# Wqkv in four chunks of 128 rows, a new lead for the first block, and new orders on all engines

## The chip, the core and the metric

The kernel runs on one core of a Trainium2 chip. A core has five engines that run their own instruction lists in order and wait for each other by semaphores: TensorE (PE, matrix products), VectorE (DVE), ScalarE (ACT), GpSimd (POOL) and SyncE (SP), which here issues all DMA transfers. The metric is the time of one execution on the device in microseconds (us), the median of several runs.

## The reference

The input x has 2048 rows of 512 bfloat16 numbers. The result is the sum of x, a sliding attention and a gated feed-forward layer, both of the normalised x:

```python
xn = _layernorm(x, axis=-1)
return x + _A_ref(xn, A_wqkv, A_wo) + _B_ref(xn, B_w_gate, B_w_up, B_w_down)
```

`_A_ref` makes Q, K and V with one weight matrix `wqkv` of 512 x 1536, splits them into 32 heads of 16 numbers, and lets each row attend to itself and seven earlier rows at a distance of two (offsets 0, 2, ..., 14). A softmax over the eight logits weighs V, and `wo` follows. `_B_ref` is `(gelu(xn @ w_gate) * (xn @ w_up)) @ w_down` with a hidden width of 1376.

## The kernel before

**Tiling.** The 2048 rows are worked in four blocks b of 512 rows, each made of four row tiles t of 128. The normalised x of a block lies transposed in `xnT`, features on partitions, so that a product takes 128 columns of a weight as the stationary side and up to 512 rows of x as the moving side. A product over the 512 features is four matrix instructions, kt = 0 to 3, one for each 128 features. PSUM has 8 banks of 512 float32 numbers a partition; every result takes a bank until ACT or DVE has read it.

**The steps of a block and their names.** A name is the step, the block, and a column group or a tile.
- Normalisation: `bnst`, `bnag`, `sub`, `sq`, `rstd`, `norm`. For the first four tiles the statistics are on DVE and the square root `sq0` to `sq3` on ACT; tile 1 has its sums on ACT (`sx1`, `negm1`, `sxx1`). Tiles 8 and later are normalised on ACT, with the power on POOL.
- Transposes: in block 0 by PE (`tpx`, line 899), read out by ACT (`evx`, line 919) and for tiles 0 and 1 half by DVE (`evy`, line 911). In the later blocks by DMA (`trx`, issued by SP).
- Q, K and V: in block 0, Q and K are made tile by tile as soon as a tile is transposed (`mma0_0`, `mmt0_t` for Q and `mmt1_t` for K, 128 columns each, line 959), V by 512 rows (`mm0_2_g`, line 1009). In the later blocks all three are `mm<b>_<which>_<g>`, by 512 rows. ACT reads them out (`evq`, `evk`, `evv`).
- Logits: DVE multiplies Q with shifted K (`pr`, line 1040) and adds (`pa`); PE sums over the numbers of a head (`er`, lines 1078 and 1085, which also makes a tail of the up projection); the softmax is `mask`, `d1` to `d6` on DVE with `exp`, `ln` and `d5` on ACT.
- The weights of attention go to DRAM and come back spread over the heads (`ss`, `sl` on SP). DVE multiplies them with shifted V (`pv`), adds (`pw`) and folds (`pz`).
- Feed-forward: `fg` and `fu` on PE (line 1221), `gelu` and `uev` on ACT, `h` on DVE.
- Output: `acc` on PE (line 1306, Wd and Wo), in the last block the part with Wo apart as `accw`; `fe` on ACT, `fin` on DVE, `sto` on SP.

**What sets the order.** Each engine's order is written out by hand in `ORDER` (line 404). `schedule` (line 207) walks through these lists with a table of costs only to give out PSUM banks and other buffers; `assign_sync` puts in the waits. An engine takes its list strictly in order, so a step that waits holds up all behind it.

**Around the change.** ACT's list begins with `c_tbl`, a square root of a constant that brings the square root's table (line 668), then `sx1 sq0 negm1 sxx1 sq1 evx0_0 evx0_1 evq0_0 sq2`. SP's begins with x of tiles 0 and 1, `ld_wq`, tile 2 of x, `ld_wk`, tile 3 of x, `ld_wv` and further x; the large load of the gate weights `ld_wg0` waits until `ld_wk` has landed (line 698), and stands on SP behind an x load that waits for PE. PE's begins with dummy products `warm0` to `warm14` on constants (line 678).

Of the kernel before, what the change touches and what calls it, by code (L numbers as in the profile page):

```python
# [21 lines left out]
    HAM_TAU=4.0,
    HAM_ENTER=0.52,
    HAM_EXIT=0.30,
)


class PeClock:

    def __init__(self, prm):  # L30
        self.tau = prm["HAM_TAU"]
        self.enter = prm["HAM_ENTER"]
        self.exit = prm["HAM_EXIT"]
        self.f = prm["PE_COLD_F"]
        self.avg = 0.0
        self.t = 0.0
        self.warm = False

    def run(self, start, dur, util):
        import math  # L40
        if start > self.t:
            self.avg *= math.exp(-(start - self.t) / self.tau)
            if self.warm and self.avg < self.exit:
                self.warm = False
            self.t = start
        left = dur
        total = 0.0
        while left > 1e-9:
            step = min(left, 0.2)
            real = step * (1.0 if self.warm else self.f)  # L50
            a = math.exp(-real / self.tau)
            self.avg = self.avg * a + util * (1.0 - a)
            if not self.warm and self.avg > self.enter:
                self.warm = True
            elif self.warm and self.avg < self.exit:
                self.warm = False
            total += real
# [78 lines left out]
class Graph:  # L136
# [70 lines left out]
    def schedule(self, orders, params=None):  # L207
        prm = dict(PARAMS)
        prm.update(params or {})
        LAT_X, LAT_S = prm["LAT_X"], prm["LAT_S"]  # L210
# [56 lines left out]
        for _ in range(len(self.tasks)):  # L267
# [23 lines left out]
            elif t.eng == "pe":  # L291
                sw = 0.0
                if t.mode is not None:
                    if pe_mode not in (None, t.mode):
                        sw = prm["PE_MODE_SWITCH"]
                    pe_mode = t.mode
                t.end = est + sw + pe_clock.run(est, t.dur, t.util)
                t.done = t.end + prm["PE_DRAIN"]
            else:
                t.end = est + t.dur  # L300
                t.done = t.end + prm["DRAIN"]
                if t.eng == "act" and t.table is not None:
                    act_table = t.table
# [85 lines left out]
    def report(self):  # L389
# [17 lines left out]
        "warm14 mma0_0 tpx0_1 mmt0_0 mmt0_1 mmt1_0 tpx1_0 mmt1_1 mmt0_2 tpx1_1 mmt1_2 mmt0_3 mmt1_3 "  # L407
        "mm0_2_2_0 mm0_2_1_0 fg0_0 mm0_2_0_0 fg0_1 fg0_2 fg0_3 fu0_0 fu0_1 mm0_2_3_0 fg0_4 fu0_2 fu0_3 fu0_4 "
        "fg0_5 mm1_1_0_0 mm1_0_0_0 fu0_5 fg0_6 er0_3 mm1_0_1_0 mm1_1_1_0 fg0_7 mm1_1_3_0 mm1_0_2_0 mm1_2_3_0 "
        "fg1_0 mm1_0_3_0 mm1_1_2_0 fg1_1 fu1_0 fu1_1 fu0_6 fu0_7 fg1_2 fu1_2 mm1_2_2_0 mm1_2_1_0 fg1_3 fu1_3 "  # L410
        "fg0_8 fg1_4 fu0_8 mm1_2_0_0 fg1_5 fg0_9 fu1_4 fu0_9 fu1_5 fg1_6 fg0_10 fu1_6 mm2_0_0_0 mm2_1_0_0 "
        "mm2_1_1_0 mm2_0_2_0 er1_3 fg1_7 mm2_0_3_0 mm2_0_1_0 fg1_8 mm2_1_3_0 mm2_2_0_0 fg2_0 mm2_1_2_0 accd2 "
        "fu1_7 accd1 mm2_2_2_0 fu1_8 acca0 fg1_10 mm2_2_3_0 accb0 fg2_1 fg2_2 accd3 fg2_3 fu2_0 fg1_9 fu2_1 "
        "mm2_2_1_0 fu2_2 fu2_3 er2_3 mm3_1_0_0 mm3_1_3_0 fu1_9 mm3_0_0_0 mm3_1_2_0 mm3_0_2_0 mm3_2_1_0 "
        "mm3_0_1_0 mm3_1_1_0 fg3_0 mm3_0_3_0 fg2_4 mm3_2_0_0 mm3_2_2_0 mm3_2_3_0 fu3_0 fu2_4 fg2_5 fg2_10 "
        "accd7 fu2_5 fg3_1 fu3_1 fg3_2 accd5 acca4 er3_3 fg2_6 accb4 accd6 fu2_6 fg2_7 fg2_8 fg3_10 fu2_7 "
        "fu3_2 fu2_8 fg3_3 fg3_4 fu3_3 fg3_5 fg2_9 fu2_9 fu3_4 fg3_6 fu3_5 fg3_7 fu3_6 fu3_7 fg3_8 fg3_9 "
        "fu3_8 accd11 acca8 accd10 fu3_9 accd9 accb8 acca12 accd13 accd14_0 accd14_1 accw14_0 accw14_1 "
        "accw13 accd15_0 accb12 accw15_0 accw12 accd15_1 accw15_1 accd15_2 accw15_2",
    "act":  # L420
        "c_tbl sx1 sq0 negm1 sxx1 sq1 evx0_0 evx0_1 evq0_0 sq2 evq0_1 evk0_0 evx1_0 sq3 evk0_1 bnst8 evx1_1 "
        "bnst9 evq0_2 evk0_2 evq0_3 evk0_3 ve8 sq6 vp8 sq4 bnag8 evv0_2_0 evv0_1_0 halo1 bnag9 evv0_0_0 va8 "
        "gelu0_0 bnst10 gelu0_2 uev0_0 bnst11 ve10 evv0_3_0 gelu0_1 vp10 gelu0_3 uev0_3 uev0_1 bnag10 "
        "evk1_0_0 evq1_0_0 gelu0_5 bnag11 gelu0_4 uev0_5 uev0_4 uev0_2 vb8 evq1_1_0 evk1_1_0 gelu0_6 gelu0_7 "
        "exp0 sub8 va10 evq1_2_0 vb10 ln0 sub11 d5_0 evk1_3_0 evq1_3_0 evv1_3_0 uev1_0 evk1_2_0 sub9 uev1_1 "
        "uev0_6 uev0_7 gelu1_1 gelu1_0 evv1_1_0 sub10 norm9 uev0_10b gelu1_3 evv1_2_0 gelu0_8 norm10 norm8 "
        "uev1_2 gelu1_2 norm11 gelu1_5 uev1_3 gelu1_4 bnst12 gelu0_9 uev0_9 uev1_5 uev0_8 uev0_10a bnst13 "
        "uev1_6 uev0_10c evv1_0_0 evq2_0_0 gelu0_10 evk2_1_0 ve12 evk2_0_0 vp12 evq2_2_0 bnag12 gelu1_6 "
        "uev1_4 evq2_3_0 gelu1_7 bnag13 evq2_1_0 halo2 evk2_3_0 exp1 bnst14 va12 bnst15 vb12 ve14 evk2_2_0 "
        "vp14 uev1_10b bnag14 ln1 uev1_7 d5_1 sub13 halv1 fe2 bnag15 uev1_8 va14 vb14 sub15 sub12 fe1 "  # L430
        "uev1_10c evv2_2_0 sub14 norm12 norm13 fe0 evv2_3_0 evv2_0_0 gelu2_2 gelu2_1 norm14 fe3 norm15 halo3 "
        "uev1_10a gelu2_0 gelu1_10 uev2_1 evv2_1_0 uev2_0 uev2_3 uev2_2 gelu1_8 uev2_10b uev2_10c gelu2_3 "
        "gelu1_9 evq3_0_0 evk3_0_0 evq3_2_0 evk3_3_0 evk3_2_0 evq3_1_0 exp2 halv2 evk3_1_0 uev1_9 evv3_0_0 "
        "evv3_3_0 ln2 evv3_2_0 evq3_3_0 d5_2 evv3_1_0 uev3_0 halv3 gelu2_5 uev2_10a gelu2_4 uev2_5 uev2_4 "
        "uev3_1 fe5 gelu2_10 gelu3_1 fe7 fe4 uev3_10c gelu3_2 gelu3_0 exp3 uev3_10b uev2_6 uev2_7 fe6 ln3 "
        "uev3_2 d5_3 uev2_8 gelu2_6 uev3_3 gelu2_7 gelu2_9 uev2_9 gelu2_8 gelu3_4 gelu3_5 uev3_5 gelu3_3 "
        "gelu3_6 uev3_6 uev3_4 uev3_7 gelu3_7 fe11 gelu3_10 fe10 gelu3_9 uev3_10a uev3_9 gelu3_8 uev3_8 fe8 "
        "fe9 fe13 fe12",
# [30 lines left out]
def d_act(n):  # L469
    return 0.10 + 0.00085 * n  # L470
# [950 lines left out]
```

## Time and profile before

| what | us |
|---|---|
| median of 3 runs (lowest, highest) | 184.19 (184.12, 184.24) |
| span of the profiled execution, first to last instruction | 182.8 |
| median less that span: what lies around it | 1.4 |
| PE busy | 178.0 |
| DVE busy | 168.8 |
| ACT busy | 129.3 |
| DMA, share of 16 engines over the span (queue 1) | 36.3% |

The page gives the span but no time of its own for the profiled execution, so the median of the runs stands for it. In a line of a timeline the first number is the start, the second the length, both in us from the span's start; then engine, line of the kernel, operation, output and input, and how many instructions are merged. Brackets name how long the engine stood idle just before and what ended it. Neighbouring instructions of an engine overlap a little at their ends, so that starts are the safer reading than lengths.

### The profile page before, as it was taken

The page shows a single profiled execution, that of the slowest core. Times are in us where ns is not written, and L with a number is a line of the kernel's source. Part 1 is how long each engine was busy: PE and PEld are TensorE (multiplying, and loading weights), DVE is VectorE, ACT ScalarE, POOL GpSimd, SP SyncE. Part 2 cuts the span into 40 slices and gives each one's busy share as a digit, 9 for nine tenths or more (in the row PEclk, how much of TensorE's full clock was granted, in tenths as well). Part 3 has the DMA queues.
Part 4 walks back from the last instruction along what each step waited for, and adds up shares of the span by engine and source line. Part 5 has one row for each costly group of instructions (what it writes and reads, how often), then busy time and mean ns, then how long its engine had stood idle before and what let it go on. Part 6 is the DMA issues. An engine that isn't in the chain of part 4 may idle for free.

```text
span 182.8 us, 2777 instructions
## 1 busy us (share of the span) xinstructions
PE 178.0 (97%) x1060; PEld 89.8 (49%) x1060; DVE 168.8 (92%) x169; ACT 129.3 (71%) x266; POOL 11.1 (6%) x23
## 2 busy tenths in 40 slices
PE   8799999999999999999999999999999999999994
PEld 2685444554444544444444555444444444444673
DVE  3769999999999999999999989999999999999932
ACT  5589977899899899869997596934396764145011
POOL 6000000104000000504000000000000000000000
PEclk9999999999999999999999999999999999999999
DMA  4999559610364000002742000136310246222333
GB/s 111 359 376 377 132 113 299 211 50 21 97 190 98 0 0 0 4 14 74 201 115 61 0 0 0 37 81 158 129 59 0 46 138 221 57 84 74 91 106 107
DMA packets 26220, 19.60 MB, mean 107 GB/s; under 512 B 13824, under 2 KB 23008, under 8 KB 26208
## 3 DMA queue, kind: packets, MB, share of 16 engines
q1 hardware_dynamic: 26208, 19.44, 36.3%
q8 instruction: 8, 0.13, 0.3%
q14 instruction: 4, 0.03, 0.1%
HBM read 14.71 MB, written 3.15 MB: 98 GB/s over the span
## 4 chain that ended last, share of the span: by engine, by line
PE 89%; DMA 8%; SPq 1%; issue 0%; DVE 0%; DVEq 0%
PE PS L1221 38%; PE PS L1306 28%; PE PS L1009 18%; DMA Wg<-in_B_w_gate_dram 5%; DMA Wqkv<-in_A_wqkv_dram 3%; PE PS L1260 2%; PE PS L1085 2%; PE PS L1078 1%; SPq L731 1%; SPq L687 0%; DVE OB L1350 0%; DVEq L376 0%
## 5 line engine op out<-in xcount | busy, mean ns | idle before, releaser
L1306 PE MATMUL PS<-Wd,HT 128*128 128x512 bf16 (+2 forms) x209 | 40.8, 345 | 0.0
L1221 PE MATMUL PS<-xnT,Wg 128*128 128x512 bf16 x160 | 39.6, 379 | 0.3 <-DMA Wg<-in_B_w_gate_dram 0.3
L1221 PE MATMUL PS<-xnT,Wu 128*128 128x512 bf16 x160 | 38.8, 379 | 0.0
L1009 PE MATMUL PS<-xnT,Wqkv 128*128 128x512 bf16 x160 | 37.8, 379 | 0.0
L1040 DVE TENSOR_TENSOR UNI<-QT,KT 128x4096 f16<-128x4096 bf16 x16 | 36.4, 2287 | 0.1
L1188 DVE TENSOR_TENSOR UNI<-VN,PT 128x4096 f16<-128x4096 bf16 x16 | 36.0, 2286 | 0.0
L1306 PEld LDWEIGHTS PS<-Wd,HT 128*128 128x128 bf16 x209 | 19.7, 98 | 19.0
L1238 ACT ACTIVATE UU<-PS 128x512 bf16<-128x512 f32 x40 | 22.8, 604 | 7.9 <-PE PS L1221 6.2
L1197 DVE TENSOR_TENSOR UNI<-UNI 128x4096 f16<-128x4096 f16 x12 | 27.4, 2286 | 0.0
L1009 PEld LDWEIGHTS PS<-xnT,Wqkv 128*128 128x128 bf16 x160 | 17.9, 114 | 16.9 <-ACT UU L1238 0.4
L1231 ACT ACTIVATE GG<-PS 128x512 bf16<-128x512 f32 x40 | 23.4, 600 | 2.5 <-DVE HT L1245 1.7
L1221 PEld LDWEIGHTS PS<-xnT,Wg 128*128 128x128 bf16 x160 | 15.4, 98 | 19.6 <-DMA Wg<-in_B_w_gate_dram 0.7
L1221 PEld LDWEIGHTS PS<-xnT,Wu 128*128 128x128 bf16 x160 | 15.7, 98 | 18.8
L1339 ACT ACTIVATE OB<-PS 128x512 bf16<-128x512 f32 x14 | 8.2, 594 | 21.8 <-PE PS L1306 21.8
L1053 DVE TENSOR_TENSOR UNI<-UNI 128x4096 f16<-128x4096 f16 x9 | 20.4, 2282 | 0.0
L1306 PE MATMUL PS<-Wo,OT 128*128 128x512 bf16 (+2 forms) x76 | 16.5, 345 | 0.0
L1245 DVE TENSOR_TENSOR HT<-GG,UU 128x1024 bf16<-128x1024 bf16 x20 | 13.6, 686 | 0.0
L832 POOL TENSOR_TENSOR sq<-ve,mhalf 128x2 bf16<-128x2 f32 x4 | 8.2, 2058 | 73.3 <-ACT ve L828 73.3
L1020 ACT ACTIVATE VN<-PS 128x512 bf16<-128x512 f32 x16 | 9.3, 594 | 2.5 <-PE PS L1009 2.5
L1306 PEld LDWEIGHTS PS<-Wo,OT 128*128 128x128 bf16 x76 | 7.2, 98 | 6.5
L1020 ACT ACTIVATE QT<-PS 128x512 bf16<-128x512 f32 x12 | 7.2, 597 | 3.2 <-PE PS L1009 3.2
L959 PE MATMUL PS<-xnT,Wqkv 128*128 128x128 bf16 x128 | 8.2, 219 | 1.2 <-DMA Wqkv<-in_A_wqkv_dram 1.0
(85 smaller groups left out, 153.9 us busy)
## 6 DMA issues: line engine op xcount, KB each, us to landing
PT<-pt_scratch SPq DMA_DIRECT2D x16, 256.0 KB, 4.0
XR<-in_A_x_dram SPq DMA_DIRECT2D x16, 128.0 KB, 2.4
out_dram<-OB SPq DMA_DIRECT2D x14, 128.0 KB, 2.0
Wqkv<-in_A_wqkv_dram SPq DMA_DIRECT2D x3, 512.0 KB, 5.6
XIN<-in_A_x_dram SPq DMA_DIRECT2D x6, 256.0 KB, 6.0
Wg<-in_B_w_gate_dram SPq DMA_DIRECT2D x1, 1280.0 KB, 8.8
Wu<-in_B_w_up_dram SPq DMA_DIRECT2D x1, 1280.0 KB, 11.6
Wd<-in_B_w_down_dram SPq DMA_DIRECT2D x1, 1280.0 KB, 7.7
```

Source lines behind the costliest of these rows:

```text
L832: "pool", "sq%d" % t, 7.0, lambda e, t=t, n=n: e.tensor_tensor(out=sq[:, t:t + n], in0=ve[:, t:t + n], in1=mhalf[:, 0:n], op=ALU.pow),
L1009: ins = e.matmul(PS[:, 512 * it.slot:512 * it.slot + 512], lhsT=wcols(which, kt, g), rhs=xnT[:, itx.slot, kt, :], start=(kt == 0), stop=(k ...
L1020: return e.activation(out=o, in_=PS[:, 512 * it.slot:512 * it.slot + 512], func=ACTF.Identity, scale=(QSC, 1.0, 1.0)[which])
L1040: return lambda e: e.tensor_tensor(out=UNI[:, it.slot, :, :], in0=bass.AP(QT, (itq.slot * 4 + g) * 512, [[NQT * 4 * 512, 128], [0, 8], [1, ...
L1053: return lambda e: e.tensor_tensor(out=UNI[:, i0.slot, :, :], in0=UNI[:, i0.slot, :, :], in1=UNI[:, i1.slot, :, :], op=ALU.add)
L1188: return lambda e: e.tensor_tensor(out=bass.AP(UNI, ito.slot * 4096, [[NUNI * 4096, 128], [2048, 2], [512, 4], [1, 512]]), in0=bass.AP(VN, ...
L1197: return lambda e: e.tensor_tensor(out=UNI[:, i0.slot, :, :], in0=UNI[:, i0.slot, :, :], in1=UNI[:, i1.slot, :, :], op=ALU.add)
L1221: ins = e.matmul(PS[0:M, 512 * it.slot:512 * it.slot + 512], lhsT=Wx[:, kt, j * 128:j * 128 + M], rhs=xnT[:, itx.slot, kt, :], start=(kt = ...
L1231: return lambda e: e.activation(out=GG[:, ito.slot, q, :], in_=PS[:, 512 * it.slot:512 * it.slot + 512], func=ACTF.Gelu_apprx_tanh)
L1238: return lambda e: e.activation(out=UU[:, ito.slot, q, :], in_=PS[:, 512 * it.slot:512 * it.slot + 512], func=ACTF.Identity)
L1245: return lambda e: e.tensor_tensor(out=HT[:, ito.slot, j - 1:j + 1, :], in0=GG[:, ig.slot, :, :], in1=UU[:, iu.slot, :, :], op=ALU.mult)
L1306: ins = e.matmul(PS[:, 512 * it.slot:512 * it.slot + CW], lhsT=(OT[:, ito.slot, q, ti * 128:(ti + 1) * 128] if kind == "o" else HT[:, ith. ...
```

## The change

Four things are changed, all in one step.

1. Wqkv is loaded in four transfers of 128 rows with all 1536 columns (`ld_w0` to `ld_w3`) in place of three of 512 rows by 512 columns. `ld_wg0` and `ld_wu0` wait for `ld_w1`.
2. For tiles 0 and 1, Q, K and V are made together, one chunk of 128 features at a time: `lk<kt>_<t>` is 12 matrix instructions of 128 columns, for three results in three banks. Tiles 2 and 3 have Q and K as before (`mmt`), and their V by 256 rows (`mmv_0`, `mmv_1`, 8 instructions of 256 columns each). ACT reads V of block 0 out in four pieces (`evv0_0`, `evv0_1`, `evv0_h0`, `evv0_h1`).
3. The costs that `schedule` uses are replaced and its model of PE's clock is dropped; this bears on the kernel only through which buffers are given out and where waits are put.
4. All engines but POOL have new orders; the set of instructions on DVE is the same as before. On ACT, `c_tbl` moves from the first place to the ninth, behind `sq2`, and `evx0_0` stands ahead of `sq1`. On SP, `ld_w0 ld_w1` follow tiles 0 and 1 of x, and `ld_x2` is the last x load ahead of the gate weights. On PE, steps of the blocks are interleaved in another way.

The core of the diff:

```diff
     "pe":
         "warm0 warm1 warm2 warm3 warm4 warm5 warm6 warm7 warm8 warm9 tpx0_0 warm10 warm11 warm12 warm13 "
-        "warm14 mma0_0 tpx0_1 mmt0_0 mmt0_1 mmt1_0 tpx1_0 mmt1_1 mmt0_2 tpx1_1 mmt1_2 mmt0_3 mmt1_3 "
-        "mm0_2_2_0 mm0_2_1_0 fg0_0 mm0_2_0_0 fg0_1 fg0_2 fg0_3 fu0_0 fu0_1 mm0_2_3_0 fg0_4 fu0_2 fu0_3 fu0_4 "
+        "warm14 lk0_0 tpx0_1 lk1_0 lk0_1 lk1_1 lk2_0 tpx1_0 lk2_1 lk3_1 tpx1_1 lk3_0 mmt0_2 mmt1_3 mmt0_3 "
+        "mmt1_2 mmv_1 fg0_0 fg0_1 fg0_2 fg0_3 mmv_0 fu0_0 fu0_1 fu0_2 fu0_3 fg0_4 mm1_0_0_0 fu0_4 mm1_1_0_0 "
...
     "act":
-        "c_tbl sx1 sq0 negm1 sxx1 sq1 evx0_0 evx0_1 evq0_0 sq2 evq0_1 evk0_0 evx1_0 sq3 evk0_1 bnst8 evx1_1 "
-        "bnst9 evq0_2 evk0_2 evq0_3 evk0_3 ve8 sq6 vp8 sq4 bnag8 evv0_2_0 evv0_1_0 halo1 bnag9 evv0_0_0 va8 "
+        "sx1 sq0 negm1 sxx1 evx0_0 sq1 evx0_1 sq2 c_tbl sq3 evx1_0 bnst8 evq0_1 evx1_1 evq0_0 bnst9 evk0_1 "
+        "sq6 evk0_3 evk0_0 evq0_2 sq4 evq0_3 evk0_2 ve8 vp8 bnag8 evv0_0 gelu0_0 bnag9 gelu0_2 sub8 gelu0_3 "
...
     "dve":
-        "sub7 pr0_1 rstd6 rstd4 norm7 norm5 norm6 pr0_0 norm4 pr0_3 pr0_2 pa0_0 pa0_1 pr1_0 mask d1_0 h0_1 "
+        "sub4 norm6 norm7 rstd4 norm5 norm4 pr0_3 pr0_1 pr0_0 pr0_2 pa0_0 h0_1 pa0_1 pr1_0 mask d1_0 rstd8 "
...
     "sp":
-        "ld_x0_0 ld_x0_1 ld_wq ld_x1_0 ld_wk ld_x1_1 ld_wv ld_x2 ld_x4 ld_x3 ld_wg0 ld_wu0 ld_wt0 ld_wt1 "
+        "ld_x0_0 ld_x0_1 ld_w0 ld_w1 ld_x1_0 ld_x1_1 ld_w2 ld_w3 ld_x4 ld_x3 ld_x2 ld_wg0 ld_wu0 ld_wt0 ld_x5 "
...
-        for i, nm in enumerate(("q", "k", "v")):
+        for i in range(4):
             def mk(i=i):
-                return lambda e: e.dma_start(
-                    Wqkv[:, :, i * 512:(i + 1) * 512],
-                    A_wqkv[:, i * 512:(i + 1) * 512].rearrange("(k p) n -> p k n", p=128))
+                return lambda e: e.dma_start(Wqkv[:, i, :], A_wqkv[128 * i:128 * i + 128, :])
...
-            t_w.deps.add(t_ld["wk"])
+            t_w.deps.add(t_ld["w1"])
...
+                def lead_mm(nm, gs, items, t, n, kts, rd, start):
+                    def f(e):
+                        ins = None
+                        for kt in kts:
+                            for (which, g, it, c) in gs:
+                                ins = e.matmul(PS[:, 512 * it.slot + c:512 * it.slot + c + n],
+                                               lhsT=wcols(which, kt, g),
+                                               rhs=xnT[:, XTI[0].slot, kt, t * 128:t * 128 + n],
+                                               start=(kt == 0 and c == 0), stop=(kt == 3 and c + n == 512))
+                        return ins
...
+                for t in range(2):
+                    its = [Item("mmt%d_%d" % (w_, t), P_ps, "qkv") for w_ in range(3)]
+                    for kt in range(4):
+                        lead_mm("lk%d_%d" % (kt, t), [(w_, g_, its[w_], 128 * g_) for w_ in range(3) for g_ in range(4)],
+                                its, t, 128, (kt,), xrd[t] + [(I_wq, kt)] + (its if kt else []), kt == 0)
```

## The prediction

> **What bounds the kernel now.** I read the page's busy times first, then the groups, PE's and ACT's first 30 us in order of time, and DVE's end.
>
> ```profile
> span 182.8 us, 2777 instructions
> PE 178.0 (97%) x1060; PEld 89.8 (49%) x1060; DVE 168.8 (92%) x169; ACT 129.3 (71%) x266; POOL 11.1 (6%) x23
> ```
>
> PE is the bound, and DVE is close behind it. PE's own timeline shows where its missing time is:
>
> ```profile
> 0.83 4.10 PE L678 MATMUL PS<-const-bfloat16-1.0 128*128 128x512 bf16 x10 [0.83 <-PEq L1406]
> 4.98 0.41 PE L899 MATMUL PS<-ident,XIN 128*128 128x128 bf16 x4
> 5.23 0.45 PE L678 MATMUL PS<-const-bfloat16-1.0 128*128 128x128 bf16 x5
> 6.65 0.39 PE L959 MATMUL PS<-xnT,Wqkv 128*128 128x128 bf16 x4 [0.97 <-DMA Wqkv<-in_A_wqkv_dram]
> 6.87 0.39 PE L899 MATMUL PS<-ident,XIN 128*128 128x128 bf16 x4
> 7.10 2.62 PE L959 MATMUL PS<-xnT,Wqkv 128*128 128x128 bf16 x44
> 9.55 0.39 PE L899 MATMUL PS<-ident,XIN 128*128 128x128 bf16 x4
> ...
> 17.17 1.04 PE L1221 MATMUL PS<-xnT,Wg 128*128 128x512 bf16 x4 [0.25 <-DMA Wg<-in_B_w_gate_dram]
> ```
>
> The reader is to see that dummy matmuls fill PE to 4.93, that the first useful product starts at 6.65 behind the Q weights, and that 44 products of 128 columns take 9.55 - 7.10 = 2.45 us, 55.7 ns each. The chain of waits gives the rate of the long ones:
>
> ```profile
> 19.07 4.32 PE PS L1221 x20
> ```
>
> That is 216 ns for each product of 512 columns. ACT's timeline holds the head of the chain that feeds PE, and a table load later on:
>
> ```profile
> 0.79 1.28 ACT L668 ACT_TABLE_LOAD   x1 [0.79 <-PEq L1406]
> 3.43 0.63 ACT L760 ACTIVATE XR<-XIN 128x512 bf16<-128x512 bf16 x1 [1.14 <-DMA XIN<-in_A_x_dram]
> 3.96 0.18 ACT L760 ACTIVATION_READ_ACCUMULATOR XR<-XIN 128x1 f32 x1
> 4.06 0.28 ACT L786 ACTIVATE sq<-mv,eps 128x1 bf16<-128x1 bf16 x1
> 5.51 0.36 ACT L919 ACTIVATE xnT<-PS 128x256 bf16<-128x256 bf16 x1
> ...
> 19.61 0.20 ACT L800 ACTIVATE vb<-s 128x2 bf16<-128x2 f32 x1
> 19.82 1.28 ACT L1231 ACT_TABLE_LOAD   x1
> 21.11 0.60 ACT L1231 ACTIVATE GG<-PS 128x512 bf16<-128x512 f32 x1
> ```
>
> The first load ends at 2.07, before x is there (3.43): it costs nothing. The one at 19.82 stands between two instructions and costs its whole 1.29 us. Last, DVE's end, from the timeline of all engines:
>
> ```profile
> 172.12 1.22 DVE L1203 TENSOR_TENSOR OT<-UNI 128x2048 bf16<-128x2048 f16 x1
> ...
> 173.65 1.51 PEld L1306 LDWEIGHTS PS<-Wo,OT 128*128 128x128 bf16 x12
> ```
>
> This is `pz3`, and after it the first product that needs it: DVE delivers 0.3 us before PE asks. A later DVE moves the end as surely as a later PE.
>
> **The change part by part.** The sum is against the profiled execution: span 182.8; the median of the three times is 184.19, so 1.4 us lie around the span, and I leave them as they are.
>
> *The head of ACT.* `c_tbl`, whose square root had the table loaded at 0.79, moves behind `sq2`. ACT's first instruction is now `sx1`, an Identity, and the built program has two loads ahead of `sq0`: one of another set before `sx1`, and one of the square root's set between `sx1` and `sq0` (eleven loads in all, ten before). The second can't start before `sx1` and its accumulator read are through, 4.14. With the 1.28 of the row, `sq0` goes from 4.06 to 5.44: +1.38. The chain behind it moves along: `norm0` 4.57 to 5.95, the transpose `tpx0_0` 4.98 to 6.36. `evx0_0` now stands ahead of `sq1` and so follows its transpose by the 0.45 that `evy0_0` had (5.43 against 4.98): 6.81, with 0.36 to 7.17. The first product `lk0_0` starts 0.07 later, 7.24 against 6.65: +0.59. The old wait for the Q weights is hidden behind this.
>
> [...]
>
> *The chunks of Wqkv.* The three loads of 512 KB become four of 384 KB in longer rows, the same bytes. The first two are issued one place earlier than K was. Ahead of chunk 0 are only 256 KB of x; K, with more in front of it, landed at 8.35. The products ask for chunk 0 at 7.24, 1 at 8.2, 2 at 10.2, 3 at 11.8: I cost it at nothing; what hides it is the later head. If a chunk were late, it costs PE its lateness, at most 1 us. `ld_x2` now waits for the transposes on SP with Wg and Wu queued behind: Wg goes out near 8.9, not 8.37. It landed at 17.13 and is asked for at 17.8: nothing, at worst 0.3.
>
> *The lead on PE.* Block 0's Q, K, V took 128 x 55.7 ns + 16 x 216 ns = 10.6 us; now 160 x 55.7 ns + 16 of 256 columns (half of 216, an estimate) = 10.65: +0.1. But the order leaves PE fewer gaps. From 6.65 to `er0_3` at 32.02 are 25.37 us; the work in them is 140 x 55.7 ns + 76 x 216 ns = 24.2, so PE stood for 1.15. In the new order I carried the three engines forward by hand with the rows' durations (512 evictions 0.5 from start to start, statistics 0.62, squares 0.70): PE waits once, 0.1, for `norm1` (sq1 7.07, norm1 done 7.94, `tpx0_1` 8.0). Then 172 x 55.7 ns + 16 x 108 ns + 64 x 216 ns = 25.1 give `er0_3` at 7.24 + 0.1 + 25.1 = 32.45, with one more group of four 512-products (0.86) done than before. So PE is 0.86 - 0.43 = 0.4 us ahead there. The covers are thin: `fg0_4` is due at 25.6 and its bank (`uev0_2`) free at 25.4; `pa0_1` is done at 32.3, just before `er0_3`. ACT stands at almost no idle from 11.6 to 40; a slip of 0.3 there costs PE 0.1 to 0.3.
>
> *DVE.* Its long stream began at `pr0_1`, 16.48. Now the evictions of Q and K end with `evk0_2`, done at 18.3, and four norms stand ahead of `pr0_3`: it begins at 18.35. In return two reciprocals and four norms (1.24 us, 18.69 to 19.67 and 21.87 to 22.13) are out of the stream, and the 0.9 us of waits that the profile names in it (0.3 for `er0_3`, 0.6 for the exponential) may go. `pz3` starts at 18.35 + (172.12 - 16.48) - 1.24 - 0.9 = 171.85 plus what DVE waits. PE, 0.4 ahead, wants it started by about 172.1. Up to 0.3 us of DVE waits are free, all above them move the end.
>
> *The orders behind it.* The instructions are the same; the waits are not. Bounds: none (the sums above), or what small misfits add up to. I carried PE's and DVE's sums through the new order without gaps: `er2_3` is due at 89.5 and its last addend `pa2_1` done at 89.0 (before: done at 87.1, asked for at 98.0); `h1_4` ahead of it asks for `uev1_9` in the moment it is ready; `d1_3` is 0.3 early for `er3_3`. The nearest rows for such misfits are the waits of DVE above, 0.3 to 0.6. I take 0.8 us on DVE or PE, 0.3 of which are free: +0.4, between 0 and 2. SP carries stores and transposes between the score loads, 0.3 to 1.3 us each; the multiplications they feed come 8.5 us and more behind the scores, as before: 0 to 0.3.
>
> Sum: +0.59 +0.1 -1.15 +0.1 = -0.4, and +0.4 for misfits: no change, 184.2.
>
> **The rivals.**
> 1. *Gapless.* All covers hold: -0.4 us, 183.8, and 183.5 with a head 0.3 quicker. For it: no engine in my sums is late by over 0.3 us. Against: six places have a slack under 0.3.
> 2. *The load is not in the way.* If `sq0` starts at 4.06 as before, `lk0_0` starts near 5.95, and 1.3 us come off the head: 182.9. Against: the built order has the load between `sx1` and `sq0`.
> 3. *Slower: DVE becomes the bound.* The place is `pa2_1` ahead of `er2_3`: PE there has nothing to cover it, and what DVE loses then is lost for `pz3` too. It decides from 1.1 us of DVE waits after 18.35 (0.3 free, 0.4 that PE is ahead, 0.4 to leave "no change"). With 2 us, as three waits of the length of those named, 184.2 - 0.4 + 1.7 = 185.5.
> 4. *Slower: PE falls back to its slow clock in the head.* Nine dummy products take 4.1 us, over 0.4 us each, twice the later 216 ns; PE warmed up at about 4.9. It now stands from 4.93 to 6.36 and again 0.35, against 0.97 at a stretch before, which slowed nothing. A fall that lasts as long as that warming, 4.1 us at half speed, costs 2.0: 186.2. [...]
>
> **How the numbers follow.** 0.2% is 0.37 us, about what a measurement of this kernel can tell from no change. No change as summed: 0.41, own range 183.85 to 184.55. Gapless 0.14, load not in the way 0.05: faster 0.19. DVE the bound or several small waits of PE 0.35, clock 0.05: slower 0.40. The range leaves out 1 in 10 on each side: down to the gapless 183.6, up to 185.6.
>
> **What would show it.** Two table loads before 5.5 us, the second 1.28 us at 4.14; `lk0_0` at 7.2; no wait of PE for Wqkv; `pr0_3` at 18.4; `er0_3` at 32.4 to 32.8; `pz3` at 172 to 173. I am wrong if `lk0_0` starts before 6.7 or after 7.6, if products near 8 us take over 60 ns each, or if PE's waits after 33 us come to more than 1 us.

## The result, and the profile after

The changed kernel takes 187.4 us (median of 4 runs, 186.25 to 187.58) against 184.22 for the kernel before on the same chip: 1.0156 times as long, 95% interval 1.0128 to 1.0184. I had forecast no change, 184.2, with a range that ended at 185.6. From the page of the profiled execution:

```profile
span 185.6 us, 2829 instructions
...
PE 177.7 (96%) x1075; PEld 92.4 (50%) x1092; DVE 169.6 (91%) x169; ACT 129.6 (70%) x267; POOL 8.4 (5%) x23
...
q14 instruction: 5, 0.04, 0.1%
```

The span grew by 2.8 us, while PE is busy 0.3 us less than before and DVE 0.8 more. The last line is from the list of DMA queues: five packets of instructions against four before; it becomes important below. ACT's timeline of the first 8 us:

```profile
0.80 1.28 ACT L713 ACT_TABLE_LOAD   x1 [0.80 <-PEq L1358]
3.71 0.63 ACT L713 ACTIVATE XR<-XIN 128x512 bf16<-128x512 bf16 x1 [1.63 <-DMA XIN<-in_A_x_dram]
4.24 0.19 ACT L713 ACTIVATION_READ_ACCUMULATOR XR<-XIN 128x1 f32 x1
4.45 1.28 ACT L739 ACT_TABLE_LOAD   x1
5.74 0.30 ACT L739 ACTIVATE sq<-mv,eps 128x1 bf16<-128x1 bf16 x1
...
7.11 0.38 ACT L872 ACTIVATE xnT<-PS 128x256 bf16<-128x256 bf16 x1
```

The second load stands where it was expected, between `sx1` and `sq0`, and takes 1.28 us with nothing behind it: 5.74 follows 4.45 + 1.28 at once. All of it is some 0.3 later than forecast, because this execution's x came 0.28 later (3.71 against 3.43). PE in the same stretch, and then, as the last line, the start of `er0_3`, the first step behind the lead:

```profile
6.68 0.40 PE L852 MATMUL PS<-ident,XIN 128*128 128x128 bf16 x4 [2.13 <-DVE mv L716]
6.91 0.45 PE L635 MATMUL PS<-const-bfloat16-1.0 128*128 128x128 bf16 x5
7.55 1.47 PE L910 MATMUL PS<-xnT,Wqkv 128*128 128x128 bf16 x12 [0.18 <-ACT xnT L872]
8.81 0.63 PE L852 MATMUL PS<-ident,XIN 128*128 128x128 bf16 x4
9.24 3.61 PE L910 MATMUL PS<-xnT,Wqkv 128*128 128x128 bf16 x48
12.69 0.39 PE L852 MATMUL PS<-ident,XIN 128*128 128x128 bf16 x4
...
34.37 0.62 PE L1030 MATMUL PS<-xnT,Wt 128*32 128x256 bf16 x16
```

PE stands 2.13 us, and then the first 12 products of the lead take 8.81 - 7.55 = 1.26 us, 105 ns each, twice the 55.7 of before; the 48 behind them average 72. The table of stretches says why. Its columns are the stretch, its length, the busy time of PE, its weight loads, DVE, ACT and POOL, then the granted clock, the DMA share and GB/s:

```profile
7.00:8.00 1.00, 0.81 (x12) 0.64 (x10) 0.62 (x4) 0.57 (x2) 0.00 (x0) 0.71 0.87 333
8.00:9.00 1.00, 1.00 (x12) 1.00 (x11) 0.27 (x1) 0.00 (x0) 0.00 (x0) 0.50 1.02 356
9.00:10.00 1.00, 1.00 (x13) 1.00 (x11) 0.52 (x2) 0.38 (x1) 0.00 (x0) 0.50 0.97 347
10.00:11.00 1.00, 1.00 (x13) 1.00 (x12) 0.93 (x4) 0.38 (x2) 0.00 (x0) 0.58 0.61 152
11.00:12.00 1.00, 1.00 (x22) 1.00 (x20) 0.96 (x3) 0.01 (x1) 0.00 (x0) 1.00 1.06 312
```

The granted clock is halved for some 3.4 us, between 7.4 and 10.8; the page's line of the clock shows no other drop while PE works, and none before the change. That column doesn't tell all, though: it reads 1.00 over the first microseconds too, where the dummy products of 512 columns start 0.43 us apart, twice the later 216 ns. Whether PE runs at its full rate is seen from the distance of its products. In this execution the full rate came at about 4.0: the eighth and ninth dummy start 0.34 and 0.22 us ahead of the next, and so the dummies end at 4.54, where those of before ended at 4.93.

The end, from the timeline of all engines, before and after:

```profile
179.88 0.39 PE L1306 MATMUL PS<-Wo,OT 128*128 128x128 bf16 x4
...
180.37 0.29 DVE L1350 TENSOR_TENSOR OB<-PS,XR 128x128 bf16<-128x128 f32 x1 [0.21 <-PE PS L1306]
```

```profile
174.43 1.22 DVE L1155 TENSOR_TENSOR OT<-UNI 128x2048 bf16<-128x2048 f16 x1
...
175.79 1.90 PE L1258 MATMUL PS<-Wo,OT 128*128 128x256 bf16 x12
...
181.91 0.39 PE L1258 MATMUL PS<-Wo,OT 128*128 128x128 bf16 x4
...
182.41 0.29 DVE L1302 TENSOR_TENSOR OB<-PS,XR 128x128 bf16<-128x128 f32 x1
```

PE's last four products start at 181.91 (179.88 before): +2.03. DVE's last sum ends at 182.70 (180.66 before): +2.04. The span grew by 2.8, so that 0.8 us arises after all engines are done with their arithmetic. Two answers on the DMA of the last 2 to 3 us, before first, then after. A line of a queue has its packets, megabytes and share of the time; a line of a store ends with the size and the time from issue to landing:

```profile
q1 hardware_dynamic: 428, 0.20, 33.9%
...
out_dram<-OB SPq DMA_DIRECT2D x1, 32.0 KB, 1.6
```

```profile
q14 instruction: 1, 0.01, 1.2%
...
out_dram<-OB SPq DMA_DIRECT2D x1, 32.0 KB, 2.3
```

The same last store of 32 KB lands 1.6 us after its issue before, and 2.3 after; and now a packet of the instruction queue goes out among the last stores.

### The profile page after: what moved, and what is told of

Read it like the earlier page. It is cut to its first block, busy times and chain, and to the rows that moved or that the text cites. A ratio compares the mean times of both kernels' runs of the same rounds, so it can differ in the third digit from the quotient of the medians.

```text
span 185.6 us, 2829 instructions
## 1 busy us (share of the span) xinstructions
PE 177.7 (96%) x1075; PEld 92.4 (50%) x1092; DVE 169.6 (91%) x169; ACT 129.6 (70%) x267; POOL 8.4 (5%) x23
## 4 chain that ended last, share of the span: by engine, by line
PE 51%; DVE 26%; ACT 14%; issue 4%; DMA 3%; SPq 0%; DVEq 0%; ACTq 0%
PE PS L1258 17%; PE PS L1173 17%; PE PS L961 8%; PE PS L910 7%; DVE UNI L1140 6%; DVE UNI L992 5%; DVE UNI L1149 4%; DVE UNI L1005 4%; ACT UU L1190 3%; ACT GG L1183 2%; DVE HT L1197 2%; DVE OB L1296 2%; DMA PT<-pt_scratch 2%; ACT XIN L806 1%; DMA XIN<-in_A_x_dram 1%
## 5 line engine op out<-in xcount | busy, mean ns | idle before, releaser
L1258 PE MATMUL PS<-Wd,HT 128*128 128x512 bf16 (+2 forms) x207 | 40.2, 345 | 0.2
L1173 PE MATMUL PS<-xnT,Wg 128*128 128x512 bf16 x158 | 38.8, 379 | 0.1
L1173 PE MATMUL PS<-xnT,Wu 128*128 128x512 bf16 x156 | 37.9, 379 | 0.3 <-issue 0.2
L961 PE MATMUL PS<-xnT,Wqkv 128*128 128x512 bf16 x137 | 34.0, 379 | 0.5 <-issue 0.2
L1190 ACT ACTIVATE UU<-PS 128x512 bf16<-128x512 f32 x40 | 23.6, 611 | 7.8 <-PE PS L1173 7.6
L1183 ACT ACTIVATE GG<-PS 128x512 bf16<-128x512 f32 x40 | 22.9, 613 | 2.6 <-DVE HT L1197 2.0
L961 PEld LDWEIGHTS PS<-xnT,Wqkv 128*128 128x128 bf16 x144 | 16.2, 114 | 15.5 <-ACT GG L1183 0.4
L910 PE MATMUL PS<-xnT,Wqkv 128*128 128x128 bf16 (+1 forms) x176 | 12.9, 238 | 0.2 <-ACT xnT L872 0.2
L910 PEld LDWEIGHTS PS<-xnT,Wqkv 128*128 128x128 bf16 x176 | 12.1, 118 | 0.6 <-ACT xnT L872 0.4
L785 POOL TENSOR_TENSOR sq<-ve,mhalf 128x2 bf16<-128x2 f32 x4 | 5.5, 1378 | 79.5 <-ACT ve L781 79.5
```

What stands on the lines that cost most here:

```text
L910: ins = e.matmul(PS[:, 512 * it.slot + c:512 * it.slot + c + n], lhsT=wcols(which, kt, g), rhs=xnT[:, XTI[0].slot, kt, t * 128:t * 128 + n ...
L961: ins = e.matmul(PS[:, 512 * it.slot:512 * it.slot + 512], lhsT=wcols(which, kt, g), rhs=xnT[:, itx.slot, kt, :], start=(kt == 0), stop=(k ...
L1173: ins = e.matmul(PS[0:M, 512 * it.slot:512 * it.slot + 512], lhsT=Wx[:, kt, j * 128:j * 128 + M], rhs=xnT[:, itx.slot, kt, :], start=(kt = ...
L1183: return lambda e: e.activation(out=GG[:, ito.slot, q, :], in_=PS[:, 512 * it.slot:512 * it.slot + 512], func=ACTF.Gelu_apprx_tanh)
L1190: return lambda e: e.activation(out=UU[:, ito.slot, q, :], in_=PS[:, 512 * it.slot:512 * it.slot + 512], func=ACTF.Identity)
L1258: ins = e.matmul(PS[:, 512 * it.slot:512 * it.slot + CW], lhsT=(OT[:, ito.slot, q, ti * 128:(ti + 1) * 128] if kind == "o" else HT[:, ith. ...
```

## The experiments

Unless told otherwise every kernel computes the whole result. "Ratio" is the time over that of the kernel before on the same chip, with its 95% interval.

### The table load

Theory: the load costs PE its own length in the head, and the stop that it makes brings the slow clock. First the changed kernel with the load back at the head of ACT's list:

```diff
-        "sx1 sq0 negm1 sxx1 evx0_0 sq1 evx0_1 sq2 c_tbl sq3 evx1_0 bnst8 evq0_1 evx1_1 evq0_0 bnst9 evk0_1 "
+        "c_tbl sx1 sq0 negm1 sxx1 evx0_0 sq1 evx0_1 sq2 sq3 evx1_0 bnst8 evq0_1 evx1_1 evq0_0 bnst9 evk0_1 "
```

> The changed kernel with c_tbl back in ACT's first place, all else of the change kept. Theory A (the second table load and the half clock that follows from PE's longer gap make up all of the loss): one load ahead of sq0, sq0 at 4.1, lk0_0 at 5.9 to 6.3, no half clock, pr0_3 near 17.5, and a time of 182.9 to 184.2, 1.3 us or more under the changed kernel's faster runs (186.25) and 3 us under its median (187.4). Theory B (the new orders behind the head are slower by themselves): the head is quicker in the same way, but the time stays at 185.5 or above, with PE waits after 33 us.

Measured: 185.09 us, ratio 1.0052 (1.0032 to 1.0072). PE, from its timeline:

```profile
4.95 0.60 PE L852 MATMUL PS<-ident,XIN 128*128 128x128 bf16 x4
...
6.10 0.88 PE L910 MATMUL PS<-xnT,Wqkv 128*128 128x128 bf16 x12
```

The lead starts at 6.10, ahead of the first product of before (6.65), and there is no drop of the clock: the four transposes are still at the half rate (0.40 us for four, from 4.95 to the next step at 5.35), the 12 products of the lead take 0.72 us to the next step, 60 ns each. So 2.3 of the 3.2 us hang on the place of one instruction (1.9 by the ratios). 0.9 us do not, though PE's last products start at 179.88 here, to the hundredth where they did before.

The other way round, the kernel before with its load late:

```diff
-        "c_tbl sx1 sq0 negm1 sxx1 sq1 evx0_0 evx0_1 evq0_0 sq2 evq0_1 evk0_0 evx1_0 sq3 evk0_1 bnst8 evx1_1 "
+        "sx1 sq0 negm1 sxx1 sq1 evx0_0 evx0_1 evq0_0 sq2 c_tbl evq0_1 evk0_0 evx1_0 sq3 evk0_1 bnst8 evx1_1 "
```

> The kernel before with only c_tbl moved behind sq2, which brings the second load ahead of sq0 there too. Theory A: sq0 at 5.5 to 5.8, the first product at 7.2 to 7.6, and PE and DVE, which had no slack behind the head, end later by as much: 185.1 to 185.6 with the full clock, 186.3 to 187.3 if PE falls to half clock in its gap. Theory B (the load costs little by itself, the orders behind it make the loss): 184.2 to 184.7.

Measured: 184.85 us, ratio 1.0042 (1.0007 to 1.0078). On ACT:

```profile
4.16 1.28 ACT L786 ACT_TABLE_LOAD   x1
5.46 0.30 ACT L786 ACTIVATE sq<-mv,eps 128x1 bf16<-128x1 bf16 x1
```

The load costs about 0.65 us at the median, close to the +0.59 of the prediction. But the five executions lie in two groups: 184.69 to 184.85, 0.5 to 0.6 above the kernel before, and 185.78 and 185.93, 1.6 and 1.7 above. The profiled one, 185.78, is of the second group. PE stood 1.46 us at a stretch in it, from 4.94 to 6.40. The clock column reads 1.00, but not so the products (stretch, length, PE's busy time and number of products, clock, DMA share, GB/s):

```profile
7.00:8.00 1.00, 1.00 (x12) 1.00 1.07 327
8.00:9.00 1.00, 1.00 (x12) 1.00 1.04 360
9.00:10.00 1.00, 1.00 (x17) 1.00 1.06 352
10.00:11.00 1.00, 1.00 (x22) 1.00 1.04 347
```

A row with 12 products of 128 columns goes with the half rate, as in the changed kernel at a clock of 0.50; one with 22 with the full rate, which comes at 9.4 here. PE had not reached it when the dummies ended, ten of them in 4.11 us, and behind the stop it took until then. So the full rate was lost in two ways around a stop in the head: in the changed kernel it fell after it had come (stop of 2.13 us), and here it came late (1.46 us). That the late rise makes up the 1.0 us between the two groups is likely but not shown, as the other four executions have no trace.

### The slow clock

Two kernels put dummy products into PE's stop and leave the load where the change has it: first eight of 512 columns and five of 128, then three of 512 alone.

```diff
-                return lambda e: e.matmul(PS[:, 512 * it.slot:512 * it.slot + n], lhsT=one_l,
-                                          rhs=one_r[:, 0:n], start=True, stop=True)
+                def f(e):
+                    for m in [n] + {9: [512] * 8, 14: [128] * 5}.get(i, []):   # second kernel: {9: [512] * 3}
+                        ins = e.matmul(PS[:, 512 * it.slot:512 * it.slot + m], lhsT=one_l,
+                                       rhs=one_r[:, 0:m], start=True, stop=True)
+                    return ins
+                return f
```

> The changed kernel with 8 more dummy products of 512 columns ahead of tpx0_0 and 5 more of 128 ahead of lk0_0, which keep PE busy in the gap; the late c_tbl and its load stay. Theory A: the products near 8 us take 56 ns each, granted clock 1.0 all along, and the time is 1.1 to 1.7 us under the changed kernel's median, 185.7 to 186.3, and not lower, since the load stays. Theory C (the half clock costs nothing because ACT or DVE is later anyway): 187.0 to 187.6.

Measured: 186.45 us, ratio 1.0121 (1.0099 to 1.0143), just above the range that was expected. The mean clock of the profiled execution was 0.998, and the 48 products behind 9.39 took 2.68 us, 56 ns each; but the dummies ran past the time when the first transpose was ready (it started at 7.52 in place of 6.68), and so most of the gain went to them.

> The changed kernel with three more dummy products of 512 columns behind the last of its warm-up products, which brings PE's stop from 2.13 us (4.54 to 6.68) to about 1.0 and leaves the head of ACT where it is, second table load included. Theory of the clock: the half clock between 7 and 11 us goes, the 48 lead products behind 9.2 us run in about 2.7 instead of 3.45 us, er0_3 starts about 1.1 us earlier (33.2 instead of 34.37) and the time is 186.3 (186.0 to 186.6). Rival, that the slow clock is hidden behind what ACT and DVE do in the head: er0_3 and the time stay at 34.4 and 187.4. If the time that the earlier run with more dummies gave (186.45) was held back by those dummies, this one is 0.2 to 0.8 below it.

Measured: 185.79 us, ratio 1.0089 (1.0067 to 1.0111). PE:

```profile
6.40 0.40 PE L856 MATMUL PS<-ident,XIN 128*128 128x128 bf16 x4 [0.41 <-DVE mv L720]
...
7.27 0.86 PE L914 MATMUL PS<-xnT,Wqkv 128*128 128x128 bf16 x12 [0.19 <-ACT xnT L876]
...
8.28 2.84 PE L914 MATMUL PS<-xnT,Wqkv 128*128 128x128 bf16 x48
10.96 0.39 PE L856 MATMUL PS<-ident,XIN 128*128 128x128 bf16 x4
...
32.64 0.62 PE L1034 MATMUL PS<-xnT,Wt 128*32 128x256 bf16 x16
```

The stop is down to 0.41 us, the clock reads 1.00 in every row from 4 to 13 us, the 48 products take 10.96 - 8.28 = 2.68 us, 56 ns each, and from the first transpose to `er0_3` it is 32.64 - 6.40 = 26.24 us against 34.37 - 6.68 = 27.69: the slow clock costs 1.45 us, shown on the same orders. The changed kernel's own executions fit this: three have a mean clock of 0.989 and take 187.36 to 187.58, the fourth has 1.000 and takes 186.25. The difference to the run with the load first, 185.79 - 185.09 = 0.70, is about the load itself once more.

### The tail: first theory

The 0.9 us that were left stood behind the last product. My first theory was the new order of the last products on PE: `accw12` ends later there, so that the 128 KB store of tile 12 goes out just ahead of the last store. Undone (with the load first), and done alone in the kernel before:

```diff
-        "accd15_1 accb12 accw15_0 accw12 accw15_1 accd15_2 accw15_2",
+        "accb12 accw15_0 accw12 accd15_1 accw15_1 accd15_2 accw15_2",
```

```diff
-        "accw13 accd15_0 accb12 accw15_0 accw12 accd15_1 accw15_1 accd15_2 accw15_2",
+        "accw13 accd15_0 accd15_1 accb12 accw15_0 accw12 accw15_1 accd15_2 accw15_2",
```

> The changed kernel with the table load first again (185.1 us in the run of that edit alone) and, beside it, the old order of the last products on PE: accd15_1 behind accw12 instead of ahead of accb12. Theory of the tail: in that earlier run the last product starts at 179.88 and the last sum ends at 180.7 as before the change, but the span is 1.1 longer, because accw12 ends later, so that the 128 KB store of tile 12 is issued right ahead of the last 32 KB store and the two land together. With the old order fin12 starts near 179.75 instead of 180.01, ahead of the end of the last product, the last store lands about 1.1 us earlier, and the time is 184.1 (183.9 to 184.4), the same as before the change. Rival, that the stores are slow for another reason (the earlier stores, the state of the queues): 185.1, with the span still 2.6 us behind the end of the last issue.

> The kernel before with one thing changed: accd15_1 ahead of accb12 on PE, as the change has it. Theory of the tail: nothing moves until 177 us, fin12 slips from 179.74 to 180.0, the last product stays at 179.88, the span grows by about 1.0 us to 183.8 and the time to 185.2 (184.9 to 185.4). Rival: 184.2, as PE does the same products in the same time and the end of the last sum does not move.

Measured: 184.77 us, ratio 1.0041 (1.0021 to 1.0061), and 184.05 us, ratio 0.9999 (0.9986 to 1.0013). The theory falls: the old order still leaves 2.9 us from the end of DVE's last sum (180.12) to the end of the span (183.0), and the new order in the kernel before leaves 2.3 (179.74 to 182.0; 2.1 in the kernel before as it is).

### The tail: an instruction fetch

The landings in the trace showed what to ask next. The trace has 16 landings for each store, which I take for its 16 parts. In the kernel before, all 16 parts of the last store land within 0.2 us. In the changed kernel 15 do, and the last part comes 0.68 us behind the fifteenth. In just this stretch an 8 KB packet of the instruction queue is under way, for 0.54 us; that it is on the DMA engine of the late part is inferred, as the trace doesn't name the engine. In the kernel before that packet goes out at 184.54, after the span's end (182.8). Both kernels have the same work on DVE, but the built program of the change has 195 instructions there and not 190: five more waits stand as instructions of their own. If the packet is a fetch of DVE's instructions and due at a fixed place of DVE's list, it comes five instructions earlier. To test it, DVE's first memset, at 0.9 us while it waits for x, is cut into six pieces in the kernel before (five more instructions, no more work), and into eleven pieces in two kernels of the change's kind:

```diff
-        G.task("dve", "c_wdz", 0.25, lambda e: e.memset(Wd[0:32, 10, :], 0.0), wr=[(I_wd, 2)], prio=PC + 1)
+        G.task("dve", "c_wdz", 0.25, lambda e: [e.memset(Wd[0:32, 10, 16 * i:16 * i + 16], 0.0) for i in range(5)] and e.memset(Wd[0:32, 10, 80:], 0.0), wr=[(I_wd, 2)], prio=PC + 1)
```

> The kernel before with five more instructions on DVE and no more work: the first memset, of 0.27 us at 0.91, is cut into six pieces, in a stretch where DVE idles 1.88 us for the first rows of x. In the traces so far the last 32 KB store of the kernel before lands on all 16 DMA engines within 0.2 us, 1.56 us after the start of its issue; of the changed kernel it lands on 15 engines in the same time and on the last one 0.68 to 0.98 us later, and an 8 KB packet of the instruction queue (0.39 to 0.75 us on one engine) stands in just these 2 us; in the kernel before it comes 1.8 us after the end of the span. The changed kernel has 195 instructions on DVE, the kernel before 190. Theory that this fetch is DVE's, due at a fixed place of its stream: here it falls among the last stores, the last landing slips by 0.7 to 0.9 and the time is 184.85 (184.6 to 185.1). Rival, that the fetch belongs to another engine or that the pieces are hidden like the memset was: 184.1, with the fetch behind the span.

> The changed kernel with the table load first and the old order of the last products (184.77 in the earlier run) and ten more instructions on DVE without more work (the first memset in eleven pieces). Theory of DVE's instruction fetch: its place in the stream comes ten instructions earlier, before the last value product of DVE ends, near 170 to 174 us, where no store of the end is under way; the last store lands on all engines together and the time is 184.0 (183.8 to 184.2), no slower than the kernel before. Rival, that the late landing is of the stores themselves: 184.77.

> The changed kernel as it is, with ten more instructions on DVE without more work (the first memset in eleven pieces). Theory of DVE's instruction fetch: it leaves the last stores, the last landing comes 0.7 us earlier and the time is 186.7 (186.4 to 186.9), with the table load and the half clock in the head as before. Rival: 187.4.

| kernel | DVE instructions | fetch goes out at | span ends | last part of the last store behind the fifteenth | time, ratio |
|---|---|---|---|---|---|
| before | 190 | 184.54 | 182.8 | 0.01 | 184.2 |
| changed | 195 | 183.48 | 185.6 | 0.68 | 187.4, 1.0156 |
| table load first | 195 | 181.45 | 183.9 | 0.98 | 185.09, 1.0052 |
| and old order of the last products | 195 | 181.22 | 183.0 | 0.83 | 184.77, 1.0041 |
| and ten more on DVE | 205 | 175.12 | 181.9 | 0.01 | 183.83, 1.0005 (0.9981 to 1.0028) |
| changed, ten more on DVE | 205 | 177.80 | 184.7 | 0.03 | 186.37, 1.0124 (1.0109 to 1.0139) |
| before, five more on DVE | 195 | 180.93 | 182.8 | 0.84 | 184.84, 1.0041 (1.0026 to 1.0056) |

A ratio is not that of the two medians: of the kernel with the load first, the old order and ten more, 4 of the 12 executions took 184.7 to 185.5 us, so that its ratio is just above 1 though its median is below the kernel before. No trace has one of these four.

The DMA of the last 2 us or so, of the kernel before with five more, then of the kernel with the load first, the old tail and ten more:

```profile
q14 instruction: 1, 0.01, 0.7%
...
out_dram<-OB SPq DMA_DIRECT2D x1, 32.0 KB, 2.4
```

```profile
q1 hardware_dynamic: 396, 0.19, 33.8%
...
out_dram<-OB SPq DMA_DIRECT2D x1, 32.0 KB, 1.6
```

The late landing comes and goes with the number of DVE's instructions: five more bring it into a kernel that computes the same in the same order, for 0.64 us, and ten more take it out again by moving the fetch to a place where no last store waits, for 0.94 and 1.0 us between the medians (0.7 and 0.6 by the ratios; the late parts themselves were 0.83 and 0.68 late). This is shown. The other traces agree: the last part is 0.75 to 0.84 late in the three further kernels with 195 instructions and 0.02 in the two with 190 and the two with 205. And the start of the packet goes with a place in DVE's list, not with the time (the table has it between 175.12 and 184.54): it goes out when DVE has started 192 of the instructions that the trace records in all seven kernels with 195, and 191 in all four with 205.

### ACT's full queue

Between 33 and 90 us the changed order loses PE some 0.5 us more than the products need, a little at a time, mostly behind ACT's queue. With the load first and the old tail I pushed statistics of tiles 12 and 13 back on ACT, and the load of Wo behind the transposes on SP:

```diff
-        "... uev1_3 bnst12 gelu1_4 gelu1_2 bnst13 uev1_5 ve12 gelu1_6 vp12 uev1_4 gelu1_5 bnag12 evq2_0_0 bnag13 uev1_6 evk2_2_0 sub12 uev1_10c va12 evq2_2_0 vb12 gelu1_7 evk2_1_0 uev1_7 ..."
+        "... uev1_3 gelu1_4 gelu1_2 uev1_5 gelu1_6 uev1_4 gelu1_5 bnst12 evq2_0_0 bnst13 uev1_6 ve12 evk2_2_0 vp12 uev1_10c bnag12 evq2_2_0 bnag13 gelu1_7 sub12 evk2_1_0 va12 uev1_7 vb12 ..."
-        "... trx4_1 sl0_2 ld_wo trx5_0 sl0_3 trx4_0 trx5_1 ss1_2 ..."
+        "... trx4_1 sl0_2 trx5_0 sl0_3 trx4_0 trx5_1 ld_wo ss1_2 ..."
```

> The run with the table load first and the old order of the last products, and two more moves aimed at PE's waits between 55 and 60 us (0.26 us on a GELU for er1_3, 0.20 us on transposed xnT): on ACT, the statistics of row tiles 12 and 13 (bnst12, ve12, vp12, bnst13, bnag12, bnag13, sub12, va12, vb12) go behind the evictions up to gelu1_5, about 4 us later; on SP, the 512 KB load of Wo goes behind the four transposes of tiles 4 and 5. Theory that ACT's queue there is what loses PE 0.4 us per stretch: PE gets 0.2 to 0.4 us back and the time is 183.8 (183.6 to 184.0) if the tail is mended too, below the kernel before. Rival, that the waits only move to later evictions, since ACT is full from 33 to 66 us: the same time as the run without the two moves, 184.1.

Measured: 185.96 us, ratio 1.009 (1.0063 to 1.0117), 1.2 us more than without the moves. The waits of PE's weight loads, first without, then with the moves:

```profile
57.67 0.34 PEld L1030 LDWEIGHTS PS<-xnT,Wt 128*32 128x32 bf16 x16 [0.74 <-ACT GG L1183]
59.26 1.44 PEld L961 LDWEIGHTS PS<-xnT,Wqkv 128*128 128x128 bf16 x8 [0.60 <-DMA xnT<-XIN]
65.45 1.41 PEld L1173 LDWEIGHTS PS<-xnT,Wu 128*128 128x128 bf16 x8 [0.45 <-ACT QT L972]
```

```profile
57.96 0.34 PEld L1029 LDWEIGHTS PS<-xnT,Wt 128*32 128x32 bf16 x16 [0.42 <-ACT GG L1182]
...
65.66 0.55 PEld L1172 LDWEIGHTS PS<-xnT,Wu 128*128 128x128 bf16 x4 [0.55 <-ACT QT L971]
66.85 0.55 PEld L1172 LDWEIGHTS PS<-xnT,Wu 128*128 128x128 bf16 x4 [0.64 <-ACT GG L1182]
67.94 0.55 PEld L1172 LDWEIGHTS PS<-xnT,Wg 128*128 128x128 bf16 x4 [0.55 <-ACT KT L971]
73.51 1.44 PEld L960 LDWEIGHTS PS<-xnT,Wqkv 128*128 128x128 bf16 x8 [0.69 <-ACT EX L1084]
```

In these traces a weight load idles 0.42 where nothing is missing (0.43 ahead of three `er` of the kernel before); what goes beyond I count as PE's loss, an estimate (0.74 - 0.42 = 0.32 ahead of `er1_3`, where PE itself stood 0.24). `er1_3` lost its wait (0.74 to 0.42) and `mm2_0_0_0` its own; four others took their place. From `er0_3` to `er1_3` PE gained 26.03 - 25.72 = 0.31 us, and from there to `er2_3` it lost 32.51 - 31.63 = 0.88. The rival is right, and the moves are worse than it said. In this execution PE also stood 0.75 us at 9.86 for the third chunk of Wqkv, ahead of the moves; so about half of the 1.2 us is not theirs. The two moves were made together, and which of them did what was not tested.

### Faster than both

From the kernel with the load first, the old tail and ten more instructions on DVE, two moves more:

```diff
-        "... er1_3 mm2_0_0_0 mm2_1_1_0 fg1_7 ..."
+        "... er1_3 fg1_7 mm2_0_0_0 mm2_1_1_0 ..."
```

> The run with ten more instructions on DVE and one more move: on PE, fg1_7 goes ahead of mm2_0_0_0 and mm2_1_1_0, so that a product that needs no new xnT stands where PE waits 0.2 us for the transposes. Theory that this wait is a matter of order: 0.1 to 0.2 us less than the run without the move. Rival, that PE is then held by the next free PSUM bank, since ACT is full there: the same or up to 0.2 more.

Measured: 183.75 us, ratio 0.9989 (0.997 to 1.0009), against 183.83 without the move: the same. From `er1_3` to `er2_3` it is 31.44 us against 31.46; the run without the move had no wait for transposes in its profile, so the move had nothing to fill. Then, on SP:

```diff
-        "... ld_w1 ld_x1_0 ld_x1_1 ld_w2 ld_w3 ..."
+        "... ld_w1 ld_x1_0 ld_w2 ld_x1_1 ld_w3 ..."
```

> The run with fg1_7 moved, and one more move on SP: the load of the third chunk of Wqkv goes ahead of the load of the second row tile's last half (ld_x1_1). In that run PE waits 0.27 us for this chunk at 9.25 (0.75 us in the run with the moves on ACT), while the statistics of ld_x1_1's rows start at 8.96 on DVE and the transposes that need them stand at 11.51 on PE, 0.7 us behind their input. Theory that the chunk's landing is what holds and scatters the lead: the wait goes, PE is 0.2 to 0.4 us earlier to the end, and the time is 183.4 (183.2 to 183.7), below the kernel before by more than its measurement is uncertain. Rival, that x1_1 is then late in its place (it would land about 1 us later, at 9.2): 183.8 to 184.2, with DVE waiting for x where PE waited for Wqkv.

Measured: 183.39 us, ratio 0.9957 (0.9941 to 0.9974): 0.4% less than the kernel before, and the interval leaves out 1. PE's lead, without the move and with it:

```profile
6.81 2.17 PE L910 MATMUL PS<-xnT,Wqkv 128*128 128x128 bf16 x36
9.25 0.86 PE L910 MATMUL PS<-xnT,Wqkv 128*128 128x128 bf16 x12 [0.27 <-DMA Wqkv<-in_A_wqkv_dram]
```

```profile
7.39 2.84 PE L910 MATMUL PS<-xnT,Wqkv 128*128 128x128 bf16 x48
```

The chunk lands at 8.26 in place of 9.20, and the wait for it is gone. In this execution it would not have come anyway, as x came 0.2 late and PE asks for the chunk only at 9.4. The runs lie between 183.26 and 183.88, where those of the two kernels ahead of it reach from 183.3 to 185.5. The profiled execution is the slowest of the five, so the shorter time is seen in the runs and not in its span; that the chunk's landing is what shortens it is argued, with intervals that just touch (the kernel ahead has 0.997 to 1.0009).

## Why the prediction was wrong

The miss is 3.2 us. PE's end moved by 2.03: 0.31 at `lk0_0`, 1.45 by the clock, 0.16 in the rest of the lead (25.37 us from `lk0_0` to `er0_3` without the clock, 25.2 forecast) and 0.14 in misfits (0.54 against the 0.4 taken) add up to 2.06 on top of a forecast of no change. The stores add 0.8, which makes the 2.8 of the spans. The rest lies in what I compared with: in the later executions of the kernel before the time is mostly 1.8 to 2.1 us above the span, not 1.4, so that its profiled execution was some 0.6 longer than the median one. Of the changed kernel the time is 1.76 above the span, 0.2 less than that. That makes 2.8 + 0.6 - 0.2 = 3.2. The excess of the profiled execution lies in its head: its first product waited 0.97 us for the Q weights and started at 6.65, `er0_3` at 31.95. In two experiments with the same head (the kernel before with the new last products, and with five more on DVE) they start at 6.33 and 6.04, and at 31.03 and 31.11, and behind `er0_3` nothing differs. The +0.59 of the prediction was counted from that late start.

- *The head of ACT*: right in kind and size. The load stands where the step put it and takes 1.28 us, with `sq0` at once behind it (5.74). `lk0_0` came at 7.55 for 7.24, 0.28 of which is the later x. The load costs 0.65 to 0.70 us between the medians in two experiments, +0.59 was the term.
- *PE falls back to its slow clock* was rival 4, with a chance of 0.05 and a price of 2.0; it happened, and costs 1.45. This is the step that failed: *The lead on PE* counted all its products at 55.7 ns, the full rate, and put the clock at nothing. Ahead of it I had read that 0.97 us of standing slowed nothing; for a longer stop no trace stood behind the chance of 0.05. Between the full rate at 4.0 and the fall at 7.4 PE was busy for 1.24 of 3.4 us. The stop was 2.13 us and not the 1.43 of the forecast, because x came 0.28 late and the dummies ended at 4.54, not 4.93. But 1.43 would not have been safe. With x in time the stop was 1.99 (the changed kernel with ten more on DVE), and the clock fell too; and with a stop of 1.46 PE stayed at the half rate up to 9.4. In the profiled executions with stops up to 0.75, and in that of before with its 0.97, PE was at the full rate by 6.9 and stayed there. A step that lengthens a stop needs its own spread, not one value.
- *The chunks of Wqkv* "cost nothing": so in the changed kernel, whose late head hides them. With the load first the lead starts at 6.10, but that the chunks are worth the difference to 6.65 is not shown, as the old loads allow 6.33 and 6.04 in other executions. The third chunk is then waited for, 0.27 and 0.75 us in two executions; the place of `ld_w2` on SP moves its landing.
- *The lead on PE* was right to 0.2 us but for the clock. *DVE* began `pr0_3` at 20.03 for 18.35, and at 18.30 in the run with three dummies, so the term was right without the slow clock. From there to `pz3` (174.43) it took 154.4 us, 0.9 more than the sum had, which counted on no wait. Even so `pz3` ends at 175.65, and PE's first product with it starts at 175.79 without a wait, so DVE isn't the bound (rival 3 falls), by a thin margin. *Rival 2* falls by the load at 4.45. *Misfits* were the right size, 0.54 us of PE, mostly behind ACT between 33 and 90 us.
- *"1.4 us lie around the span, and I leave them as they are"*: this is the term that was missing. I had treated the instructions of DVE as unchanged because the set of operations is, and the stores' end as a constant. Five waits became instructions, a fetch slid from behind the last landing to ahead of it, and 0.7 to 1.0 us appeared where no engine works.

Two executions of the changed kernel with ten more on DVE kept a clock of 0.998 and more and took as long as the two at 0.990 (186.2 to 186.4); there is no trace of them, and what they lost stays open. A late rise like that of the kernel before with its load late would fit: there the mean clock is 0.999, with PE at the half rate up to 9.4. What sets the moments of the rise and of the fall stays open as well.

## What to carry to other kernels

Look at the longest stop of PE in the head (0.97 us slowed nothing here, 1.99 and 2.13 went with a fall of the clock), and at the distance from product to product, not only at the column of the clock, which read 1.00 with the dummies at half rate. Three dummy products of 512 columns, which ended before the real ones started, cost nothing here and saved 1.45 us up to `er0_3`, while eight, with five short ones, made the first transpose 0.84 us later. A table load belongs where its engine waits anyway: the one at 0.80 ended at 2.08, ahead of x at 3.71, and the one ahead of `sq0` cost 0.65 to 0.70 us. And the first place on the list counts: `sx1` had no load of its own behind `c_tbl` in the kernel before, and had one, the one at 0.80, when it came first. When the last store lands late for no reason on any engine, look at the list of queues for an instruction packet among the last transfers: ten more small instructions early on DVE moved it here and took 0.6 to 1.0 us off.

## What the runs showed of the hardware that I had not expected

- PE's granted clock fell to 0.50 for 3.4 us, from 7.4 to 10.8, after a stop of 2.13 us; PE was busy for 36% of the 3.4 us ahead of the fall (1.24 of 3.40). It was back at 1.00 by 11.0, with PE busy all the time from 8.0 on. In both traces with a fall it came 3.4 us after the full rate had come (from 4.0 to 7.4, and from 3.8 to 7.2).
- The moment of the full rate differs from execution to execution though the dummies start at 0.83 or 0.84 in all: 3.8, 4.0, 5.05, 5.6, 6.2, 6.8 and, with a stop of 1.46 us, 9.4. The clock column reads 1.00 ahead of it; only the products, 107 ns and not 56 apart, show the half rate.
- Packets of instructions go out on DMA queues of their own beside the data (five on one queue in the page of the changed kernel, four before). No wait in these traces points to one in the middle of the kernel; at the end, with one 8 KB packet of 0.3 to 0.75 us under way, one of the 16 parts of the last store landed 0.68 to 0.98 us behind the others.
- Work that was moved off ACT's full queue was not gone: 0.31 us won up to one wait behind ACT came back as 0.88 us in four others.
